# Sigmoid attention and a gated feed-forward block on one core: how fast the weight-block sums are emitted, and which engines finish the last tile

## The chip, the cores and the metric

The kernel runs on one core of a Trainium2 chip. The core has a matrix engine (TensorE, "PE" in the profile), three engines for elementwise work (VectorE or DVE, ScalarE or ACT, GpSimd or POOL), a SyncE queue (SP) that issues transfers, and 16 DMA engines. The metric is the device time of one execution in microseconds, the median of three runs: 426.59 us before the change (426.4 to 428.45). The profiled execution spans 425.0 us, and all times in views of the trace count from its start.

## The reference

```
scores = q @ k^T / sqrt(64) - log(448)          # 8 x 12 heads, 448 x 64 each
x      = sigmoid(scores) @ v                    # 3584 tokens x 768 after the heads are joined
g, val = x @ w_gate, x @ w_val                  # 768 -> 1536
out    = (g * sigmoid(g) * val) @ w_out         # 1536 -> 768
```

Inputs and output are float32. There is no row sum as in softmax: every score passes through a sigmoid by itself.

## The kernel before

**Attention.** The 96 heads are cut into 24 units of four heads (`NQ`), three units for each of eight batch entries. For each unit q and k are loaded in float32 to staging buffers `st`, cast to bfloat16 by GpSimd (`src`, line 231), transposed by DMA (`qkT`, line 380), multiplied on TensorE (`ps_sc`, line 397, in bursts of two score tiles, eight small matmuls), sent through the sigmoid on ScalarE (`pt`, line 414), and multiplied with v (`ps_pv`, line 432). The results are evicted as `xT`, two feature blocks a unit, by VectorE or ScalarE.

**First feed-forward half.** For batch entry b and each of twelve 128-wide blocks f, `f1` computes a gate product `ps_g` and a value product `ps_v` (six matmuls each, line 472). ScalarE takes the sigmoid of the gate (`s`, line 478), VectorE multiplies it with the gate (`t`, line 482), and VectorE multiplies the value product with that into `hT` (line 488). Both products draw on the same two PSUM buffers, tag "G": the next gate product waits for `t` of the block before, the next value product for its `hT`.

**Second feed-forward half.** Pairs of batch entries (m) are done together, seven token tiles t for each. Three pairs of tiles use a form with seven products instead of eight (`f2_set`, Strassen's idea on 2 x 2 blocks, steps 1 to 7, products `ps_o` of six matmuls at line 651, combined by VectorE at line 656). It needs sums of blocks of hT (lines 631 to 637 and 692) and sums of blocks of the output weights: `weight_sums`, twelve VectorE subtractions of 128 x 768 float16 at line 593, done once and kept in staging buffers. They read weights that GpSimd has cast (`wo16`, line 338). The seventh tile is done plainly (`f2`, line 543). Its last half, for the last m, is cut into two parts of 192 columns, n = 0 and n = 1.

**What sets the order.** The program first emits operations in a list. Each unit has four quarters (`sl`); in each quarter the loop emits the score bursts, feed-forward blocks and other work due. From the second half of unit 8 on, it emits `WSN` weight sums in each quarter, and a second-half step is emitted only once the last sum, ("ws", 4, NH - 2), is in the list. A planner, `list_schedule`, then gives each engine an order: it takes, engine by engine, the first operation in a window of the list whose inputs and buffers are ready by the planner's own durations, and buffers of a tag are handed out in the order of the list. What comes out is a fixed order for each engine. On the chip an engine goes through its order strictly, waiting on semaphores, so a waiting instruction holds up everything behind it on that engine.

**The end.** In the last tile, part n = 0 (columns 384 to 575) is evicted by VectorE (line 550), and its two row blocks are stored from SyncE and from GpSimd. Part n = 1 is evicted by ScalarE (line 548) and stored from SyncE and ScalarE (all at line 557). At line 887 every engine drains, and the engines meet.

Of the kernel before, what the change touches and what calls it, by code (L numbers as in the profile page):

```python
# [153 lines left out]
def kernel(  # L154
# [10 lines left out]
    nc = tc.nc  # L165

    B, H, S, D = q.shape
    DM = H * D
# [30 lines left out]

    NCW = 4  # L200
    NEARLY = 5
    WSN = 2
    CW = DFF // NCW
    FC = CW // 128
    wg16 = [one.tile([128, KC, CW], FP16, tag=f"wg{c}", name=f"wg16_{c}") for c in range(NCW)]
# [14 lines left out]
    def op(*a, **kw):  # L220
        o = Op(*a, **kw)
        ops.append(o)
        return o
# [294 lines left out]
    def f2(m, u, final=False):  # L518
        t, half = divmod(u, 2)
        end = m == B // 2 - 1 and t == NS - 1  # L520
        if end and half:
            w = DM // 4
            parts = [("A", slice(2 * w, 3 * w)), ("TO", slice(3 * w, 4 * w))]
        else:
            w = DM // 2
            parts = [("A" if final and u % 4 < 2 else "TO", slice(half * w, half * w + w))]
        a = [f2_part(m, u, final, end, n, *p) for n, p in enumerate(parts)]
        R.setdefault(("f2", m), []).extend(a)

    def f2_part(m, u, final, end, n, tag, cs):  # L530
        t, half = divmod(u, 2)
        w = cs.stop - cs.start

        def fpe():
            if half == 0:
                T["osb", m, t] = sb.tile([128, DM], FP32, tag="osb", bufs=slots["osb"], name=f"osb_{m}_{t}")
            if tag == "A":
                o = psum.tile([128, 2, 512], FP32, tag="A", bufs=2, name="ps_ol")[:, 0, 0:w]
            else:
                o = psum.tile([128, w], FP32, tag="TO", bufs=2, name="ps_o")  # L540
            T["o", m, u, n] = o
            for f in range(NF):
                nc.tensor.matmul(out=o, lhsT=T["hT", m][:, f, t * 128:(t + 1) * 128],  # L543
                                 rhs=wo16[:, f, cs], start=(f == 0), stop=(f == NF - 1))

        def fe():
            if half == n:
                nc.scalar.activation(out=T["osb", m, t][:, cs], in_=T["o", m, u, n], func=COPY, scale=HREC)
            else:
                nc.vector.tensor_scalar_mul(T["osb", m, t][:, cs], T["o", m, u, n], HREC)  # L550

        def fo(c, blocks, dma):
            def fn():
                for k in blocks:
                    bb, s = divmod(2 * t + k, NS)
                    rows = slice((2 * m + bb) * S, (2 * m + bb + 1) * S)
                    dma.dma_start(out=out[rows, c].rearrange("(p s) d -> s p d", s=NS)[s],  # L557
                                  in_=T["osb", m, t][64 * k:64 * k + 64, c])
            return fn
        a = op("PE", 1.95 * w / (DM // 2), fpe,  # L560
               deps=[(R["hT", 2 * m + 1, f], 0.16 * f) for f in range(NF)] + [R["wo16", f] for f in range(NF)],
               take=[tag] + (["osb"] if half == 0 else []))
        if half == 0:
            R["osb", m, t] = a.got("osb")
        e = op("ACT" if half == n else "DVE", 0.1 + 0.35 * w / (DM // 2), fe, deps=[a], give=a.got(tag))
        R["o", m, u] = e
        give = R["osb", m, t] if half and (n or not end) else []
        if end and n:
            op("SP", 0.5, fo(cs, [0], nc.sync), deps=[e], give=give)
            op("ACT", 0.5, fo(cs, [1], nc.scalar), deps=[e])  # L570
        elif end:
            op("SP", 0.5, fo(cs, [0], nc.sync), deps=[e])
            if half:
                op("POOL", 0.5, fo(cs, [1], nc.gpsimd), deps=[e])
            else:
                op("SP", 0.5, fo(cs, [1], nc.sync), deps=[e])
        elif half == 1:
            op("SP" if final else "POOL", 1.1, fo(slice(0, DM), [0, 1], nc.sync if final else nc.gpsimd),
               deps=[e, R["o", m, u - 1]], give=give)
        return a  # L580
# [199 lines left out]
    for i in range(NQ + QB + 2):  # L780
        att = i < NQ
        for sl in range(4):
# [11 lines left out]
            if i > WO + 4 or i == WO + 4 and sl > 1:  # L794
                for _ in range(WSN):
                    next(wsums, None)
# [41 lines left out]
            while f2q and f2acc >= f2q[0][0] and ("ws", 4, NH - 2) in R:  # L838
                w, fn = f2q.pop(0)
# [13 lines left out]
    end = 0.0  # L853
    warm_now = True
    for o in list_schedule(ops, {**slots, "st": before}, window):
        warm_now = warm_now and o is not R["cool"]
        if o.eng == "PE":
            if warm_now and o is not warmup and o.t0 - end > FILL:
                fill(int((o.t0 - end - FILL) / 0.215) + 1)
            end = o.t0 + o.dur  # L860
# [31 lines left out]
```

## Time and profile before

| what | value |
|---|---|
| median device time | 426.59 us |
| span of the profiled execution | 425.0 us |
| TensorE busy | 412.4 us (97%) |
| VectorE / ScalarE / GpSimd busy | 229.1 / 219.3 / 132.2 us |
| share of TensorE on the chain that ended last | 88% |
| stretch 88 to 97 us: TensorE busy | 9.00 of 9.00 us |
| stretch 97 to 103.5 us: TensorE busy, VectorE busy | 4.30 and 6.50 of 6.50 us |
| stretch 103.5 to 404 us: TensorE busy | all of it |
| the twelve weight sums, line 593 | 91.6 to 105.2 us; 542 to 1277 ns each |

The busy columns are averages over stretches with different limits; where TensorE is not busy, the list of waits tells which engine it waited for, and the timeline tells what that engine was doing. In a timeline, the bracket at a line's end is the idle time before the group and who ended it. Durations of successive instructions overlap a little, so the step from one start to the next is the time that one takes.

### The profile page before, as it was taken

To read this page: it belongs to the slowest core of one execution; us is meant where nothing else is said; L and a number is where in the kernel's file an instruction comes from. 1 tells how busy PE (TensorE), PEld (TensorE's weight loads), DVE (VectorE), ACT (ScalarE), POOL (GpSimd) and SP (SyncE) were. 2 spreads that over 40 slices of the span, in tenths; PEclk is the share of its full clock that TensorE was granted. 3 is DMA by queue.
4 is the path that set the end of the run, shared out by engine and by line. 5 is a ranking of instruction groups with operands and counts; after the bars stand their busy time and mean duration, and the time that the engine had idled before them with its cause. 6 is when DMAs were issued, how large, how long until landed. Compare 5 with 4: busy or idle time off the path is not lost.

```text
span 425.0 us, 7958 instructions
## 1 busy us (share of the span) xinstructions
PE 412.4 (97%) x3217; PEld 207.4 (49%) x3217; DVE 229.1 (54%) x400; ACT 219.3 (52%) x293; POOL 132.2 (31%) x195
## 2 busy tenths in 40 slices
PE   8989899997999999999999999999999999999996
PEld 3444444443554554554454544545444545555554
DVE  3544444469664754654474564555455474673772
ACT  6987578665445456355645546544745552112000
POOL 1788855767132322314304314224100001000000
PEclk9999999999999999999999999999999999999999
DMA  8999969997815664574753835747301102021054
GB/s 280 378 375 375 374 191 343 328 317 203 247 53 87 161 143 121 160 134 151 175 126 94 203 52 197 174 80 179 72 2 37 39 2 75 2 74 39 0 149 113
DMA packets 64580, 66.97 MB, mean 158 GB/s; under 512 B 35536, under 2 KB 60688, under 8 KB 64544
## 3 DMA queue, kind: packets, MB, share of 16 engines
q1 hardware_dynamic: 62704, 59.29, 48.6%
q0 software_dynamic: 1760, 7.13, 6.7%
q8 instruction: 25, 0.41, 0.4%
q14 instruction: 11, 0.09, 0.1%
q10 hardware_dynamic: 80, 0.05, 0.1%
HBM read 47.19 MB, written 11.01 MB: 137 GB/s over the span
## 4 chain that ended last, share of the span: by engine, by line
PE 88%; DMA 7%; DVE 1%; POOL 1%; ACT 1%; issue 1%; POOLq 0%; SPq 0%
PE ps_g L472 24%; PE ps_v L472 22%; PE ps_o L651 16%; PE ps_sc L397 8%; PE ps_pv L432 6%; DMA st<-in_moe_w_val_dram 4%; PE ps_ol L651 4%; PE ps_vl L472 3%; DMA st<-in_q_dram 3%; PE ps_o L543 2%; PE ps_ol L543 2%; POOL v L231 1%; ACT pt L414 1%; PE ps_tr L355 1%; DVE st L593 1%
## 5 line engine op out<-in xcount | busy, mean ns | idle before, releaser
L414 ACT ACTIVATE pt<-ps_sc,sbiast 128x896 f16<-128x896 f32 x168 | 159.2, 1007 | 32.0 <-PE ps_sc L397 32.0
L472 PE MATMUL ps_g<-xT,wg 128*128 128x448 f16 x576 | 124.3, 353 | 1.7 <-DVE t L482 1.6
L478 ACT ACTIVATE s<-ps_g 128x448 f16<-128x448 f32 x96 | 52.3, 545 | 127.8 <-PE ps_g L472 126.6
L472 PE MATMUL ps_v<-xT,wv 128*128 128x448 f16 x504 | 109.7, 353 | 0.6 <-DVE hT L488 0.6
L482 DVE TENSOR_TENSOR t<-ps_g,s 128x448 f16<-128x448 f32 x96 | 59.9, 624 | 91.7 <-ACT s L478 91.7
L472 PEld LDWEIGHTS <-wg 128*128 128x128 f16 x576 | 54.5, 98 | 57.1 <-issue 10.9
L472 PEld LDWEIGHTS <-wv 128*128 128x128 f16 x576 | 52.6, 98 | 58.6 <-issue 16.6
L231 POOL CAST src<-st 128x896 bf16<-128x896 f32 (+1 forms) x43 | 40.1, 932 | 104.2 <-DMA st<-in_q_dram 73.5
L488 DVE SCALAR_TENSOR_TENSOR hT<-ps_v,t 128x448 f16<-128x448 f32 x84 | 52.4, 624 | 34.6 <-PE ps_v L472 33.8
L231 POOL CAST v<-st 64x448 f16<-64x448 f32 (+1 forms) x72 | 43.6, 605 | 32.2 <-issue 15.5
L397 PE MATMUL ps_sc<-qkT 64*64 64x448 bf16 x672 | 51.3, 360 | 2.1 <-ACT pt L414 1.6
L651 PEld LDWEIGHTS <-hT 128*128 128x128 f16 x360 | 35.2, 98 | 25.6
L667 POOL DMA_DIRECT2D out_dram<-osb x32 | 16.7, 526 | 83.0 <-DVE osb L656 83.0
L229 DVE CAST xT<-ps_pv 128x448 f16<-128x448 f32 x40 | 23.5, 621 | 26.1 <-PE ps_pv L432 26.1
L432 PE MATMUL ps_pv<-pt,v 64*64 64x448 f16 x672 | 37.1, 350 | 0.4 <-ACT pt L414 0.4
L656 DVE SCALAR_TENSOR_TENSOR osb<-ps_o,osb 128x384 f32<-128x384 f32 x56 | 30.2, 552 | 6.0 <-PE ps_o L651 6.0
L651 PE MATMUL ps_o<-wo,hT 128*128 128x384 f16 x168 | 31.9, 326 | 0.0
L397 PEld LDWEIGHTS <-qkT 64*64 64x64 bf16 x672 | 14.8, 105 | 31.5 <-issue 27.4
L432 PEld LDWEIGHTS <-v 64*64 64x64 f16 x672 | 19.6, 107 | 14.3 <-issue 3.4
L557 POOL DMA_DIRECT2D out_dram<-osb x5 | 2.6, 521 | 65.2 <-DVE osb L550 65.0
L651 PE MATMUL ps_o<-st,hT 128*128 128x384 f16 x120 | 22.8, 326 | 0.0
L651 PE MATMUL ps_o<-st,s 128*128 128x384 f16 x120 | 22.8, 326 | 0.0
(45 smaller groups left out, 213.7 us busy)
## 6 DMA issues: line engine op xcount, KB each, us to landing
st<-in_q_dram SPq DMA_DIRECT2D x24, 448.0 KB, 4.4
st<-in_v_dram SPq DMA_DIRECT2D x24, 448.0 KB, 5.5
st<-in_k_dram SPq DMA_DIRECT2D x23, 448.0 KB, 4.8
out_dram<-osb POOLq DMA_DIRECT2D x36, 192.0 KB, 3.1
st<-in_moe_w_gate_dram SPq DMA_DIRECT2D x12, 384.0 KB, 8.8
st<-in_moe_w_val_dram SPq DMA_DIRECT2D x12, 384.0 KB, 8.8
st<-in_moe_w_out_dram SPq DMA_DIRECT2D x12, 384.0 KB, 6.7
out_dram<-st SPq DMA_DIRECT2D x16, 192.0 KB, 2.7
```

The costliest lines, as they stand in the source:

```text
L229: nc.vector.tensor_copy(out=o, in_=i)
L231: nc.gpsimd.tensor_copy(out=o, in_=i)
L397: nc.tensor.matmul(out=sc[64 * (g ^ a):64 * (g ^ a) + 64, a, 0:S].rearrange("k (s p) -> k s p", s=NS), lhsT=kT[r, s, 64 * g:64 * g + 64], ...
L414: nc.scalar.activation(out=pt, in_=T[("sc",) + key][:, :, 0:S], func=SIGM, bias=sb_t, scale=qkscale)
L432: nc.tensor.matmul(out=T["pv", i, a][64 * g:64 * g + 64, :], lhsT=T["v16", i][r, a, s, :], rhs=T["pt", i, s][r, a, :], start=(s == 0), sto ...
L472: nc.tensor.matmul(out=T[nm, b, f], lhsT=w[c][:, j, ff * 128:(ff + 1) * 128], rhs=T["xT", b, j], start=(j == 0), stop=(j == KC - 1))
L478: nc.scalar.activation(out=t, in_=T["g", b, f], func=SIGM)
L482: nc.vector.tensor_tensor(out=t, in0=T["g", b, f], in1=T["s16", b, f], op=MULT)
L488: nc.vector.scalar_tensor_tensor(out=T["hT", m][:, f, o * S:(o + 1) * S], in0=T["v", b, f], scalar=HSC, in1=T["t1", b, f], op0=MULT, op1=MULT)
L543: nc.tensor.matmul(out=o, lhsT=T["hT", m][:, f, t * 128:(t + 1) * 128], rhs=wo16[:, f, cs], start=(f == 0), stop=(f == NF - 1))
L651: nc.tensor.matmul(out=T["p", m, k, n], lhsT=lhs()[:, x], rhs=rhs(x), start=x == 0, stop=x == NH - 1)
L656: C[name] = op("DVE", 0.45, lambda: nc.vector.scalar_tensor_tensor(out=c(*dst), in0=T["p", m, k, n], scalar=HREC, in1=c(*other), op0=MULT, ...
```

## The change

Two things are changed. `WSN` goes from 2 to 1, so the twelve weight sums are emitted one in each of twelve quarters of units instead of two in each of six; the aim is to spread them over VectorE's other work. As the second feed-forward half is emitted only when the last sum is in the list, its first steps move later in the list. At the end of the kernel, VectorE evicts the last 192 columns in place of ScalarE, and the second row block of the columns before them is stored from ScalarE's queue in place of GpSimd's; the aim is that GpSimd has no transfer at the end.

```diff
-    WSN = 2
+    WSN = 1
...
         def fe():
-            if half == n:
+            if half == n and not (end and n):
                 nc.scalar.activation(out=T["osb", m, t][:, cs], in_=T["o", m, u, n], func=COPY, scale=HREC)
             else:
                 nc.vector.tensor_scalar_mul(T["osb", m, t][:, cs], T["o", m, u, n], HREC)
...
-        e = op("ACT" if half == n else "DVE", 0.1 + 0.35 * w / (DM // 2), fe, deps=[a], give=a.got(tag))
+        e = op("ACT" if half == n and not (end and n) else "DVE", 0.1 + 0.35 * w / (DM // 2), fe, deps=[a], give=a.got(tag))
...
             if half:
-                op("POOL", 0.5, fo(cs, [1], nc.gpsimd), deps=[e])
+                op("ACT", 0.5, fo(cs, [1], nc.scalar), deps=[e])
```

## The prediction

> **What bounds the kernel now.** I read the busy times first, then TensorE's waits, then the timelines around the waits, then the end.
>
> ```profile
> PE 412.4 (97%) x3217; PEld 207.4 (49%) x3217; DVE 229.1 (54%) x400; ACT 219.3 (52%) x293; POOL 132.2 (31%) x195
> ```
>
> TensorE is busy for 97%, and the change neither adds nor removes a matmul. So only TensorE's idle time, and what follows its last matmul, can be gained. Its waits between 85 and 115 us:
>
> ```profile
> engine line waited for: us in total, times, longest us
> PE ps_g L472 <- DVE t L482: 1.6, 1, 1.6
> PE ps_v L472 <- DVE hT L488: 0.6, 1, 0.6
> ```
>
> The same list over 106 to 425 us is empty. The reader is to see that 2.2 us, behind VectorE, is all the waiting that lies near the weight sums, and that nothing later waits, so a shift here reaches the end undiminished unless a new wait arises. TensorE and then VectorE in that stretch (start, length, group, idle before it):
>
> ```profile
> 97.05 1.31 PE L472 MATMUL ps_v<-xT,wv 128*128 128x448 f16 x6
> 99.97 1.29 PE L472 MATMUL ps_g<-xT,wg 128*128 128x448 f16 x6 [1.60 <-DVE t L482]
> 101.19 0.38 PE L397 MATMUL ps_sc<-qkT 64*64 64x448 bf16 x4
> 102.17 1.29 PE L472 MATMUL ps_v<-xT,wv 128*128 128x448 f16 x6 [0.59 <-DVE hT L488]
> ```
>
> ```profile
> 94.72 0.55 DVE L593 TENSOR_TENSOR st<-wo 128x768 f16<-128x768 f16 x1
> 96.61 2.24 DVE L593 TENSOR_TENSOR st<-wo,st 128x768 f16<-128x768 f16 x2 [1.34 <-POOL wo L338]
> 98.77 0.61 DVE L229 CAST xT<-ps_pv 128x448 f16<-128x448 f32 x1
> 99.31 0.61 DVE L482 TENSOR_TENSOR t<-ps_g,s 128x448 f16<-128x448 f32 x1
> 99.84 1.74 DVE L593 TENSOR_TENSOR st<-wo 128x768 f16<-128x768 f16 x2
> 101.50 0.61 DVE L488 SCALAR_TENSOR_TENSOR hT<-ps_v,t 128x448 f16<-128x448 f32 x1
> ```
>
> VectorE stood for 1.34 us at a sum whose weight block GpSimd had not cast, then did two sums in 2.24 us; the `t` that frees the gate's PSUM buffer was queued behind them and ended at 99.9, where TensorE goes on. Two more sums (1.74 us) then held up `hT`. The end, by the instructions of line 887 and the last issues:
>
> ```profile
> 420.57 0.52 POOL L557 DMA_DIRECT2D out_dram<-osb  x1 [64.97 <-DVE osb L550]
> 420.91 0.33 ACT L548 ACTIVATE osb<-ps_o 128x192 f32<-128x192 f32 x1 [1.49 <-PE ps_o L543]
> 421.27 0.57 ACTq L557 DMA_DIRECT2D out_dram<-osb  x1
> ...
> L887 POOLq DRAIN  x1: 3639/3639/3639, 420.5 to 420.5; - x1
> ...
> L887 SPq DRAIN  x2: 7/10/13, 423.7 to 423.8; - x2
> ...
> L887 POOLq EVENT_SEMAPHORE  x1: 17/17/17, 424.2 to 424.2; - x1
> ```
>
> SyncE, which waits for the last stores, is through at 423.8. GpSimd's drain runs from 420.5 for 3.64 us to 424.2, and only then do the engines meet: GpSimd ends the kernel, not the last store.
>
> **What the Trainium skill says.** "SBUF — State Buffer", section "Who interferes with whom": a VectorE instruction with two SBUF inputs contends with a GpSimd instruction that reads SBUF, and the one that comes later is blocked. The sums have two SBUF inputs and GpSimd casts beside them; the trace agrees, since a sum takes 542 ns at best and 1277 ns at worst. "DMA: Bandwidth & Descriptors", section "Issuing engines are not separate DMA queues": issuing elsewhere saves only the issuing engine's time. The trace agrees: the last GpSimd store lands 1.9 us after issue, ScalarE's 2.1. So I expect nothing from the transfer itself, only from GpSimd's drain.
>
> **Part 1, one sum a quarter: the sequence on TensorE.** The order of the built program shows that TensorE's order differs only from about 93 us to about 157 us of the trace, and is the same before and after that. The first difference: the product with v of unit 8 (`ps_pv`) moves one feed-forward block later. I call the blocks a (value product at 92.62), b, c and d. Step lengths, from start to start in TensorE's timeline: value before gate 1.15 (89.74 to 90.89), gate 1.22 (90.89 to 92.11), burst of eight 0.50, value before `ps_pv` 1.24, `ps_pv` 1.45 (93.86 to 95.31), burst of four 0.30. New sequence: value a 92.62; gate b 93.77; burst 94.99; value b 95.49; `ps_pv` 96.73; gate c 98.18; burst of four 99.40; value c 99.70; next product 100.85. Before, the next product after value c started at 103.30. Without a wait the gain is 2.45 us; the 2.19 of the bracketed idle time and the rest, 0.26, for the ends of matmuls that the two stops expose.
>
> **VectorE in the new order.** Its new order is: sum, t a, sum, hT a, three sums, t b, sum, hT b, sum, xT, t c. A step of t, hT or xT takes 0.54 (99.31 less 98.77). A sum takes 0.78, the mean of the twelve (4.5 + 4.5 us over twelve, in the groups of the stretch 88 to 106 us), since GpSimd casts through nearly all of it. From 91.63: sum to 92.4; t a needs the sigmoid that ends at 92.76, so to 93.34; sum to 94.12; hT a to 94.66; three sums to 97.0; t b to 97.54, due 98.18 for gate c; sum to 98.3 (its weight block was cast by 96.6, so it does not wait); hT b to 98.86, due 99.70; sum to 99.64; xT to 100.17; t c to 100.71, due 100.85 for gate d. All in time, the last just so. With all sums at the 1.2 us of the worst ones the same count ends with gate c 1.1 late, hT b 0.2 late, and t c 1.1 late: the gain is gone. At the best 0.55 there is slack everywhere. I take 0.25 us of waiting, the gain then 2.2, between 0 and 2.45. After block c there is one sum a block of 2.9 us, or two, beside 1.1 to 2.2 us of other steps; no wait there.
>
> **What moves later.** The first second-half products go from 103.3 us to about 127, and units 10 and 11 of the attention come earlier: first burst at 108.4 instead of 123.2, and about 118.5 instead of 139.5. Their inputs: the transposes were issued at 92.4 and 102.4 and land 4.9 us later by the median, so both are there. ScalarE does 2.44 us per block of 2.88, as it did from 63 to 92 us without a wait. To catch up, the new order has five second-half products in a row with two PSUM buffers ("TO"). Each lasts 0.97 and frees its buffer after one or two VectorE steps of 0.47; by the same counting each is freed some 0.3 us or more before it is needed. The second pair of tiles writes into an output buffer (three in all) that the first pair's store must have left: the store is issued near 142.5, lands 2.6 to 6.4 us later (GpSimd stores of 120 to 160 us), and the write is due at 147.8, with 2 us before TensorE needs that buffer's product gone. I count nothing, hidden by TensorE's own work. Switches between score and feed-forward work number 45 in both orders, so no cost.
>
> **Part 2, the end.** ScalarE's eviction took 331 ns, VectorE's of the same shape 358: 0.03 later. Its two stores then wait on another engine, as SyncE's did (about 0.03 from eviction to issue in both). ScalarE issues two stores, 0.57 each, the first near 420.3, so the second is not delayed. GpSimd has no store since 355 us, so its drain should be over long before; SyncE then ends last, at 423.8 plus 0.05 instead of 424.2. Gain 0.3; bounds 0 (the drain waits for something else) and 0.45.
>
> **Sum.** 426.59 - 2.2 - 0.3 = 424.1.
>
> **The rivals.** *VectorE still blocks* (the sums cost near 1 us each, t c is late): half the 2.45 stays, 426.59 - 1.2 - 0.2 = 425.2. For it: three sums now stand in a row ahead of t b, and GpSimd's casts lie beside them. Against it: margins of 0.1 to 0.8 at mean cost. *The cluster takes it back*: seven second-half products close together each wait 0.3 for their PSUM buffer, 2.1 us, and only the end is gained: 426.3. For it: margins of 0.3. Against: in the last 20 us such products run back to back without a wait, though with four buffers. *Slower*: sums at 1.2 give no gain, and both the output buffer's store (3 us late after heavy transfers) and the cluster wait (2.1 us), 426.6 + 5.1 - 2.2 that overlaps = 429.5. For it only that two costs unseen before add up; no transfer is queued there.
>
> **How the numbers follow.** Main case 0.62, VectorE still blocks 0.22, cluster 0.12, slower 0.04. Range: low 426.59 - 2.45 - 0.45 - 0.2 of measurement = 423.5; high 425.7, which takes in the second case and leaves out cluster and slower. Half a per cent is 2.13 us, the bound 424.46. Of the main case, spread over about 423.5 to 424.8, some five sixths lie below it: 0.53, and a little of the second: 0.55 faster. Slower by over 0.5%: 0.04. Within: 0.41.
>
> **What would show it.** Right: TensorE's waits of 1.6 and 0.6 us on VectorE near 100 us are gone or under 0.5 in sum, no waits in 105 to 160, the long GpSimd drain starts long before the end, and SyncE is the last. Wrong: a wait of a gate product on `t` near 98 or 101 us, sums over 1 us, `ps_o` waiting on line 656, or a drain of GpSimd that still ends at the last.

## The result, and the profile after

The changed kernel takes 423.14 us (median of five, 422.6 to 423.85). The kernel before, run in alternation with it, took 427.67 (426.4 to 428.45): ratio 0.9898, 95% interval 0.9873 to 0.9924. A second comparison gave 0.9922 (0.9897 to 0.9948; 423.25 us). The forecast was 424.1, with 423.5 as its lower end; the gain was under-sized. By their ratios the two comparisons give 4.4 and 3.3 us, and part of that distance can be the draw of runs of the kernel before: of 51 later runs of it, the ten with a mean granted TensorE clock of 0.994 to 0.996 have a median of 427.72 us and the 41 at 0.998 or more one of 426.71, and how many of the five runs behind 427.67 were of the first kind is not on record.

The two profiles, cut at four marks on TensorE: the value product of block a (92.62 before, 92.12 after), the attention product behind which both orders are the same (157.23, 154.21), the last twelve matmuls (419.72, 416.70), and the end of the span (425.0, 421.4).

| stretch | before | after | gain |
|---|---|---|---|
| start to value product of block a | 92.62 | 92.12 | 0.50 |
| to the attention product at 157 / 154 | 64.61 | 62.09 | 2.52 |
| to the last twelve matmuls | 262.49 | 262.49 | 0.00 |
| to the end of the span | 5.28 | 4.70 | 0.58 |

The list of TensorE's waits over 85 to 425 us is empty after the change; it held 2.2 us before. TensorE's timeline after the change, at blocks b and c:

```profile
96.24 1.52 PE L432 MATMUL ps_pv<-pt,v 64*64 64x448 f16 x28
97.69 1.31 PE L472 MATMUL ps_g<-xT,wg 128*128 128x448 f16 x6
98.93 0.38 PE L397 MATMUL ps_sc<-qkT 64*64 64x448 bf16 x4
99.24 1.31 PE L472 MATMUL ps_v<-xT,wv 128*128 128x448 f16 x6
100.39 1.30 PE L472 MATMUL ps_g<-xT,wg 128*128 128x448 f16 x6
```

No line carries a bracket: each product starts as the one before it leaves. VectorE's timeline beside it:

```profile
94.01 1.66 DVE L593 TENSOR_TENSOR st<-wo 128x768 f16<-128x768 f16 x2
95.59 1.17 DVE L593 TENSOR_TENSOR st<-wo,st 128x768 f16<-128x768 f16 x1
96.68 0.61 DVE L482 TENSOR_TENSOR t<-ps_g,s 128x448 f16<-128x448 f32 x1
97.22 0.64 DVE L593 TENSOR_TENSOR st<-wo,st 128x768 f16<-128x768 f16 x1
97.78 0.61 DVE L488 SCALAR_TENSOR_TENSOR hT<-ps_v,t 128x448 f16<-128x448 f32 x1
98.31 0.64 DVE L593 TENSOR_TENSOR st<-wo 128x768 f16<-128x768 f16 x1
98.87 0.61 DVE L229 CAST xT<-ps_pv 128x448 f16<-128x448 f32 x1
99.61 0.62 DVE L482 TENSOR_TENSOR t<-ps_g,s 128x448 f16<-128x448 f32 x1
```

The three sums in a row took 2.7 us, more than the 2.3 that I counted, and `t` of block b ended at 97.3, 0.4 ahead of the gate product at 97.69. `t` of block c ended at 100.2, ahead of 100.39. At the sum of 97.22 nothing waits for a cast. Before the change, too, three sums stood between the `hT` of block a and the `t` of block b, at 94.72 and 96.61, and they took 2.7 us of VectorE's time as well. So the row ahead of this `t` did not become shorter by a sum: what is gone from it is the stop of 1.34 us, and the `xT` (0.54 us), which now comes behind. The end, by the instructions of line 887 (duration in ns, start of the first and last):

```profile
L887 POOLq DRAIN  x1: 4691/4691/4691, 352.0 to 352.0; - x1
...
L887 SPq DRAIN  x2: 7/10/13, 420.6 to 420.7; - x2
...
L887 POOLq EVENT_SEMAPHORE  x1: 17/17/17, 420.7 to 420.7; - x1
```

GpSimd's long drain now runs from 352.0 to 356.7, behind its last store, and SyncE, done with the last stores at 420.7, ends the kernel.

### The profile page after: what moved, and what is told of

Its sections match the earlier page's. It is cut to its first block, busy times and chain, and to the rows that moved or that the text cites. A ratio compares the mean times of both kernels' runs of the same rounds, so it can differ in the third digit from the quotient of the medians.

```text
span 421.4 us, 7959 instructions
## 1 busy us (share of the span) xinstructions
PE 412.1 (98%) x3215; PEld 208.0 (49%) x3217; DVE 229.5 (54%) x401; ACT 218.8 (52%) x292; POOL 130.0 (31%) x194
## 4 chain that ended last, share of the span: by engine, by line
PE 89%; DMA 9%; SPq 1%; POOL 0%; issue 0%; DVE 0%; POOLq 0%
PE ps_g L472 25%; PE ps_v L472 23%; PE ps_o L651 16%; PE ps_sc L397 8%; PE ps_pv L432 6%; DMA st<-in_moe_w_val_dram 4%; DMA st<-in_q_dram 4%; PE ps_ol L651 4%; PE ps_vl L472 3%; PE ps_o L543 2%; PE ps_ol L543 2%; SPq L261 1%; PE ps_tr L355 0%; POOL src L231 0%; DVE osb L550 0%
## 5 line engine op out<-in xcount | busy, mean ns | idle before, releaser
L231 POOL CAST v<-st 64x448 f16<-64x448 f32 (+1 forms) x72 | 41.4, 575 | 25.8 <-issue 15.7
L667 POOL DMA_DIRECT2D out_dram<-osb x32 | 16.7, 526 | 90.4 <-DVE osb L656 90.4
L651 PEld LDWEIGHTS <-s 128*128 128x128 f16 x144 | 14.1, 98 | 10.2
```

The costliest lines, as they stand in the source:

```text
L231: nc.gpsimd.tensor_copy(out=o, in_=i)
L651: nc.tensor.matmul(out=T["p", m, k, n], lhsT=lhs()[:, x], rhs=rhs(x), start=x == 0, stop=x == NH - 1)
```

## The experiments

The theory: VectorE's weight sums, stopped by an uncast weight block and then done in a row, hold up the steps that free PSUM buffers, and GpSimd's drain holds up the end. The rivals: the later place of the second-half steps gains; the end alone gains more than its drain; or the loads of the first 50 us, which the change does not touch, happened to fall well.

**Only the sums one a quarter.**

```diff
-    WSN = 2
+    WSN = 1
```

> Only the sums go to one a quarter; the end is as before. Theory 1 (VectorE no longer blocks near 100 us): TensorE waits of 1.6 and 0.6 us near 100 us are gone, gain 2.4 us or a little more, about 424.2 beside a before of 426.6. Theory 2 (most of the 4.5 us comes from the end, or from loads that happen to differ): gain 1 us or less.

423.78 us beside 426.82, ratio 0.9932 (0.9917 to 0.9947): 2.9 us. No waits of TensorE from 85 us on; the stretch from block a to the attention product is 62.09 again, and the end 5.25 (417.15 to 422.4), as before the change. The sums are the larger part of the gain.

**Only the end.** All hunks of the change but `WSN`.

> Only the end is changed; the sums go two a quarter. Theory 1 (GpSimd's drain ended the kernel): from the start of the last group of twelve matmuls to the end of the span 4.7 us instead of 5.3, gain 0.4 to 0.6 us in the whole, waits near 100 us as before (2.2 us). Rival (the end is worth over 1 us): gain 1 to 2 us.

426.28 us beside 426.82, ratio 0.9988 (0.9978 to 0.9997): 0.5 us. From the last twelve matmuls to the end 4.75 (419.35 to 424.1). TensorE's waits from 85 us on stay:

```profile
PE ps_g L472 <- DVE t L482: 2.1, 2, 1.7
PE ps_v L472 <- DVE hT L488: 0.6, 1, 0.6
```

The reader is to see a third wait here (two on `t`, 2.1 us in sum, the longest 1.7): it lies at 106.9, behind a weight sum and two sums of hT blocks. The profile of before did not show it.

```profile
106.90 1.29 PE L472 MATMUL ps_g<-xT,wg 128*128 128x448 f16 x6 [0.45 <-DVE t L482]
```

**Second-half steps later, sums in pairs as before.**

```diff
-            while f2q and f2acc >= f2q[0][0] and ("ws", 4, NH - 2) in R:
+            while f2q and f2acc >= f2q[0][0] and ("ws", 4, NH - 2) in R and (i, sl) >= (11, 1):
```

> Sums two a quarter as before, end as before, but the second-half steps are held back to the quarter in which the change first lets them go. Theory 1 (the spacing of the sums is what counts): the waits near 100 us stay, 2 us or more, no gain over 0.5 us. Rival (moving the second-half steps later is what gains): waits gone, gain of 2 us or more.

427.36 us beside 426.82, ratio 1.0007 (0.9997 to 1.0018). TensorE waited 2.2 us on `t` (two waits) and 0.6 on `hT`, the stretch is 65.34. The later place of the second-half steps gains nothing; this rival falls.

**The kernel before once more.** No edit.

> The kernel before once more, for a second profile. Theory 1 (the wait of VectorE for the cast of the weights hangs on how the loads fall, so it differs from run to run): the waits near 100 us differ from 2.2 us by 0.5 us or more, and with them the time. Rival (the scatter of 2 us comes from the load-bound first 50 us): waits of 2.2 us again within 0.2, and the first 88 us differ.

Ratio 1.0003 (0.9991 to 1.0014). The waits were 1.7 and 0.6 us, within 0.1 of the first profile, and the stretch 64.74; but block a began at 91.77 instead of 92.62. Over eleven of the profiles, of kernels whose orders do not differ before 90 us, this mark lies between 91.6 and 92.6, whatever the change. In each of the thirteen profiles it comes 28.95 to 28.97 us after a value product that starts at 62.6 to 63.7 us, so this scatter of 1.0 us arises before 64 us, in a part that begins with loads that keep the DMA engines busy (80% or more over the first 50 us); that the loads are its cause is not shown. It is only a part of the whole: 51 runs of before spread from 425.5 to 429.0. The first theory of this run (the waits themselves scatter) falls for the two waits near 100 us; the third wait above does come and go.

**The order of weight loads and casts.** Every engine's order stays that of before; only which weight block a load and cast carries is changed, so that the first eight sums do not need the last three casts.

```diff
-    NCW = 4
+    NCW = 4; WORD = [0, 1, 6, 7, 2, 3, 8, 9, 4, 5, 10, 11]
...
-                for f in range(3 * (i - WO - 1), 3 * (i - WO)):
+                for f in WORD[3 * (i - WO - 1):3 * (i - WO)]:
...
-                    for f in range(3 * (i - WO), 3 * (i - WO + 1)):
+                    for f in WORD[3 * (i - WO):3 * (i - WO + 1)]:
```

> The kernel before with the order of every engine unchanged; only which of the twelve output-weight blocks is loaded and cast first is permuted, so that the first eight sums need none of the last three casts. Theory 1a (the stop of VectorE for an uncast block is over half of the cost): the stop of 1.34 us is gone, TensorE's waits near 100 us fall from 2.2 us to 0.9 or less, gain 1.3 us or more. Theory 1b (the sums in pairs beside GpSimd's casts cost it anyway): waits stay at 1.5 us or more, gain under 0.8 us.

425.55 us beside 427.0, ratio 0.9968 (0.9956 to 0.9979): 1.4 us. VectorE's timeline, in which the stop of 1.34 us before these two sums is gone:

```profile
94.04 0.54 DVE L593 TENSOR_TENSOR st<-wo 128x768 f16<-128x768 f16 x1
94.50 2.01 DVE L593 TENSOR_TENSOR st<-wo,st 128x768 f16<-128x768 f16 x2
96.43 0.61 DVE L229 CAST xT<-ps_pv 128x448 f16<-128x448 f32 x1
96.96 0.61 DVE L482 TENSOR_TENSOR t<-ps_g,s 128x448 f16<-128x448 f32 x1
97.49 1.35 DVE L593 TENSOR_TENSOR st<-wo 128x768 f16<-128x768 f16 x2
```

No wait is left at block c's gate product, though `xT` still stands ahead of block b's `t`: without the stop there is no such wait. TensorE's waits fall to 1.0 us, of which 0.8 lies at 105.49, behind a weight sum and two sums of hT blocks:

```profile
97.62 1.29 PE L472 MATMUL ps_g<-xT,wg 128*128 128x448 f16 x6
...
105.49 1.29 PE L472 MATMUL ps_g<-xT,wg 128*128 128x448 f16 x6 [0.82 <-DVE t L482]
```

The gain is the one that Theory 1a asked for, the waits are a little over its 0.9. The stretch from block a to the attention product is 63.63 here, 64.84 on the mean of four profiles with pairs (before twice, the end alone, the store alone), and 62.09 with single sums. So the stop for the cast was a little under half of the cost of the pairs, 1.2 of 2.75 us by this one profile. The rest, by difference, is put down to sums ahead of due steps, as the two waits left here show them.

**Three sums a quarter.**

```diff
-    WSN = 2
+    WSN = 3
```

> Three sums a quarter instead of two, end as before. Theory 1 (sums in a row before a step that frees a PSUM buffer cost TensorE time): two more sums of 0.8 to 1.1 us stand ahead of the gate's step, waits near 100 us rise from 2.2 us to 3.5 us or more, 1 us slower or more. Rival (the amount in a row does not matter, only the stop for the cast): waits stay within 0.5 us of 2.2, no change.

426.64 us beside 427.0, ratio 0.9991 (0.9976 to 1.0006). Against the theory: one wait of 1.9 us, no more, and a stretch of 64.11. This is what the rival forecast, but its reason, that only the stop for the cast counts, does not hold: with the stop gone in the run before, 1.5 us of the stretch were still to gain. VectorE's timeline shows why the time did not rise:

```profile
96.76 2.24 DVE L593 TENSOR_TENSOR st<-wo,st 128x768 f16<-128x768 f16 x2 [1.34 <-POOL wo L338]
98.92 0.55 DVE L593 TENSOR_TENSOR st<-wo 128x768 f16<-128x768 f16 x1
99.39 0.61 DVE L482 TENSOR_TENSOR t<-ps_g,s 128x448 f16<-128x448 f32 x1
```

One more sum stands ahead of `t`, but at 0.55 us, and `xT` (0.54) moved behind it, so `t` comes at about the same time: 6.9 us after the start of block a's value product, beside 6.7. The number in a quarter by itself is not the cost; what stands ahead of the due step is.

**Sums in pairs, begun two quarters later.**

```diff
-            if i > WO + 4 or i == WO + 4 and sl > 1:
+            if i > WO + 4:
```

> Two sums a quarter as before, but begun two quarters later in the list; end as before. The planner then gives VectorE nearly the same order over the first seven sums as in the changed kernel, and pairs after that. Theory 1 (what counts is that no sum stands ahead of a due step for long): waits near 100 us 0 to 0.8 us, gain 1.6 to 2.6 us. Rival (one sum a quarter is needed): waits of 1.5 us or more, gain under 1 us.

424.16 us beside 427.0, ratio 0.9942 (0.992 to 0.9963): 2.5 us. VectorE's order over the first seven sums is that of the changed kernel here, with three sums in a row ahead of block b's `t`. One wait of 0.3 us is left, behind a pair of sums; the stretch is 62.51:

```profile
93.59 1.37 DVE L593 TENSOR_TENSOR st<-wo 128x768 f16<-128x768 f16 x2
94.89 1.17 DVE L593 TENSOR_TENSOR st<-wo,st 128x768 f16<-128x768 f16 x1
95.98 0.61 DVE L482 TENSOR_TENSOR t<-ps_g,s 128x448 f16<-128x448 f32 x1
...
100.31 1.29 PE L472 MATMUL ps_g<-xT,wg 128*128 128x448 f16 x6 [0.27 <-DVE t L482]
```

So one sum a quarter is not needed: pairs in this order spare all but 0.4 us. That no sum stops for a cast is not enough by itself, as the 63.63 of the permuted casts shows; the order must also bring each due step in time.

**Only the store moved, ScalarE evicts as before.**

```diff
-                op("POOL", 0.5, fo(cs, [1], nc.gpsimd), deps=[e])
+                op("ACT", 0.5, fo(cs, [1], nc.scalar), deps=[e])
```

> Only the store of the last tile is moved from GpSimd's queue to ScalarE's; ScalarE evicts the last columns as before, sums two a quarter. Theory 1 (GpSimd's drain is the whole gain of the end): from the last group of twelve matmuls to the end of the span 4.7 us as in the run with the whole end changed, gain about 0.5 us. Rival (VectorE's eviction has a part): 4.9 to 5.2 us.

426.09 us beside 427.0, ratio 0.9978 (0.9967 to 0.999): 0.9 us, its interval overlapping that of the whole end. From the last twelve matmuls to the end 4.73 (419.37 to 424.1), as with the whole end changed.

**The changed kernel once more.** No edit.

> The changed kernel once more, for its size. If the gain is the sum of the two parts measured one by one (2.9 us for the sums, 0.5 to 0.9 for the end): 3.4 to 3.8 us, ratio 0.991 to 0.992, and the stretch from the value product of block a to the attention product at 154 us 62.1 us again, the end 4.7 us again. If the first comparison's 4.4 us holds: ratio 0.990 or less, and one of these stretches differs from that of the first profile.

423.25 us beside 426.69: ratio 0.9922 (0.9897 to 0.9948), 3.3 us, just under the 3.4 to 3.8 us that the parts give together, and not the 4.4 us of the first comparison. The stretch from block a to the attention product is 62.09 again; that from the attention product to the last twelve matmuls is 262.49, as in every other profile to 0.01, and the end 4.67.

**The changed kernel with the permuted casts** (the edits of both).

> The changed kernel with the permuted order of weight loads and casts of the earlier run. Theory 1 (no sum waits for a cast any more in the changed kernel): nothing is left to gain, same time within 0.3 us as the changed kernel. Rival (some executions still wait there): faster by 0.3 us or more.

423.19 us, ratio 0.9915 (0.9894 to 0.9936): the same as the changed kernel; with no stop for a cast in that kernel's profile either, nothing is left to gain from the casts there.

**One sum a quarter and only the store moved.**

> One sum a quarter and the store on ScalarE's queue, but ScalarE evicts the last columns as before. Theory 1 (VectorE's eviction gives nothing): same time within 0.2 us as the changed kernel, end 4.7 us. Rival: the end is longer by 0.1 us or more.

423.06 us, ratio 0.9919 (0.9893 to 0.9944); stretch 62.09, end 4.67. VectorE's eviction in the change gives nothing and costs nothing that these runs can tell apart.

## Why the prediction was too small

The mechanism held at each step: the two waits on VectorE went, nothing new waited, and GpSimd's drain left the end. What failed is the size of two terms of the sum, the waiting in part 1 and the gain of the end, and the allowance for scatter, all in the same direction. The low end of the range took 2.45 and 0.45 us as the most that the two parts could give; the runs gave 2.75 and 0.54.

- **"I take 0.25 us of waiting, the gain then 2.2."** There was no waiting. The stretch shrank by 2.52 us, against the 2.45 of the count without waits. The average sum in the stretch 88 to 106 us cost 0.74 us (3.6 + 3.0 over nine). The 0.78 that was counted is the mean length of one; the division given for it, 4.5 + 4.5 over twelve, is 0.75. Nor did GpSimd cast through nearly all of the stretch: it did nothing from 98.4 to 100.2 us. `t` of block c came 0.16 us before it was due, 0.14 in the count, so the count was right and the allowance on top of it was the mistake. So was taking the waits of one profile for those of every execution: the runs with the end alone, the store alone and the late second-half steps each show a second wait on `t`, of 0.4 to 0.6 us. The mean of the four pair profiles gives 2.75 us for this part, and the times of the run with only the sums changed give 2.9.
- **"Gain 0.3; bounds 0 and 0.45"** for the end. From the last twelve matmuls to the end, the seven profiles with GpSimd's store at the very end have 5.20 to 5.29 us, 5.25 on the mean, and the six without it 4.67 to 4.75, 4.71 on the mean: 0.54. The drain's lead over SyncE was 0.4, as read. The rest is small pieces that I did not count, as far as readings to 0.1 us tell: SyncE was through 3.9 us after the start of the last twelve matmuls instead of 4.0, and what follows the last arrival took 0.7 us instead of 0.8. The later eviction by VectorE, for which I took off 0.05, does not show.
- **"0.2 of measurement."** Too narrow. The kernel before was taken at 426.59, but its runs spread over 3.4 us; the start of block a alone scatters by 1.0 us. In the two profiles compared, 0.50 of the 3.6 us between the spans lies there, and the change did not make it. With the sizes above the sum is 426.59 - 2.75 - 0.54 = 423.3, near 423.14 and 423.25. That it comes so near is in part luck: from the later medians of the kernel before, 426.7 to 427.0, the same sum gives 423.4 to 423.7, and the 0.2 to 0.6 us below that are not placed.

The parts counted at nothing were rightly so. Seven second-half products close together ran without a wait; the write that needs the first pair's output buffer began at 147.12 us, with no idle time before it. The earlier attention units found their inputs there. The rival of a VectorE that still blocks fell: a sum of over 1 us, listed as a sign of being wrong, did come, with 1.17 us, but only one in the row ahead of block b's `t`, and `t` was still in time. The rivals of the cluster and of a slower kernel fell with the empty list of waits.

One part of the reasoning was incomplete without harm: I gave the 2.45 us to the spacing of the sums as one thing. The permuted casts show that a little under half came from VectorE's one stop at a sum whose weight block was cast too late.

## What to carry to other kernels

On an engine that works in order, look for what stands ahead of the step that frees a buffer of the busiest engine: work without a deadline should not stand there while its own input is still on the way, nor for longer than the step can wait. Here a change of which input arrives first cured nearly half of the loss with no change in any order, and a row of three sums did no harm where the step behind it still came in time. When the busiest engine has no waits after the changed stretch, a gain there can reach the end whole, as it did here. Ask also which engine arrives last at the final meeting of the engines: it need not be the one with the last transfer.

## What the runs showed of the hardware

GpSimd's drain at the end took the same 3.64 us (3639 to 3641 ns) in all seven profiles of kernels with a GpSimd store at the very end, for example in the run with three sums:

```profile
L887 POOLq DRAIN  x1: 3641/3641/3641, 419.9 to 419.9; - x1
```

In the kernel before it ended 1.7 us after that store had landed (issued at 420.57, landed 1.9 later). In the six profiles whose last GpSimd store lies some 70 us before the end it took 4.68 to 4.71 us, in the changed kernel from 352.0 us on. What sets these lengths stays open; moving the store to another queue takes the drain off the end either way.
